# Retention with a snake feed-forward layer: one table for all steps, and the second projection of blocks 1 to 8 as seven products of quarters

## The chip, the cores and the metric

The kernel runs on 1 core of one Trainium2 chip. The metric is the device time of one execution in microseconds (us). Three runs of the kernel before took 311.48, 315.2 and 309.82 us, so the median is 311.48.

In this text TensorE (PE in the profile) does the matmuls, VectorE (DVE), ScalarE (ACT) and GpSimd (POOL) the rest, SyncE (SP) issues most transfers. PSUM is the memory that matmuls write, in eight banks of 128 partitions x 512 f32; SBUF is the working memory.

## The reference

The first part is causal retention per batch (8) and head (8) over 576 positions with 64 columns per head; the second a feed-forward layer over all 4608 rows.

```
scores = (q @ k.T) / sqrt(64)
rel = pos[:, None] - pos[None, :]
Dmat = where(rel >= 0, gamma[head] ** rel, 0)       # gamma = 1 - 2 ** (-5 - head)
x = ((scores * Dmat) @ v), heads side by side       # (4608, 512)
h = x @ w_in                                        # w_in (512, 2048)
s = sin(alpha * h)
g = h + s * s / (alpha + 1e-9)
out = g @ w_out                                     # w_out (2048, 512), out f32
```

## The kernel before

**Blocks.** The 4608 rows are nine blocks of 512. Blocks 0 to 7 are the first 512 positions of one batch each; block 8 gathers the last 64 positions of all eight batches (class `Ends`, L427).

**Retention of a block** (class `Attention`, L240). q, k and v come in two parts of 256 positions each (`load`, L109; 0.5 MB each, issued by SP; k and v of batches 5 to 7 in four DMAs a part). `cast` (L132) scales by powers of gamma and writes f16. q and k are turned, on TensorE with `turn`/`take` (L195, L208) in batches 0 and 1, by a transposing DMA (`crossed`, L187) in the others. A part has two chunks of 128 positions. `outer` (L269) makes each chunk's sum of k x v, `take_sum`, `evict` or `evict_bank` copy it out of PSUM, `more` (L320) and `to_state` (L315) carry the state from chunk to chunk. `scores` (L332), `masked` (L350), `values` (L362) and `add_states` (L395) make the rows of a part, `keep` (L413) copies them to the block's f16 tile `xT`. The matmuls here are 64x64 tiles that share the array. The two halves of `values` take turns at a PSUM bank; between them stands a marker instruction on another engine (`told`, L234).

**Feed-forward of a block.** Units are the 16 slices of 128 of the 2048 columns. `project` (L511) makes one unit of h: four matmuls, 512 columns each, into one bank. `sine` (L524) is ScalarE's activation from that bank, `square` (L532) runs on ScalarE, VectorE or POOL, `product` (L541) is VectorE's `g = ss * (1/alpha) + h`, reading the bank again, into the tile `gT` (f16, two buffers). So a bank of h is free only after `product`.

The second projection is `gemm2` (L557). Of its 16 row-and-quarter steps per block, four make one chunk of 128 output rows: 16 matmuls of 128x128 weights (a piece of `gT`) and 512 columns of `w_out`, accumulated in one bank. `finish` (L551) copies the chunk to SBUF and issues two stores.

```
def gemm2(n, u, tag, cols=slice(0, 512)):
    c, part = divmod(u, 4)
    ...
    for fk in range(4 * part, 4 * part + 4):
        matmul(
            ops[n, c, cols.start][:, cols], gT[n][:, fk, c * P : (c + 1) * P], w_out16[:, fk, cols],
            start=(fk == 0), stop=(fk == FC - 1), skip_group_check=True,
        )
```

The inner part of the loop from block 3 on (`todo` and `after` hold the retention steps and loads of each unit):

```
for u in range(16):
    project(n, u, next(h))
    sine(n, u)
    for f in todo.get(u, []):
        f()
    ...
    elif u % 4 == 3:
        gemm2(n - 1, u, "op")
        finish(n - 1, u // 4)
        square(n, u, A_)
        product(n, u)
    else:
        square(n, u, A_ if A and u in (ON_A if n < 4 else (4, 5, 8, 9, 10)) else V)
        product(n, u)
        gemm2(n - 1, u, "op")
```

**Order.** Every engine runs its instructions in the order in which the program issues them, and the order is written by hand (`with tc.manual_schedule()`, L619). Up to block 2 it is a straight list of calls; from block 3 on a loop over units (L1104 to L1191) runs `project(n, u)`, `sine`, `square`, `product` and one step of `gemm2(n - 1, u)`, with the next batch's retention and loads hung in at fixed units. After the loop the last block's second projection stands alone, its last chunk in two column pieces, copied by ScalarE and VectorE and stored through two queues. PSUM banks are named: `h0`, `h1`, `h2` for units, `op` for output chunks, `m0` and `m1` (two banks each) for retention and, early on, for units.

**Start.** The weights (4 MB each in f32) come through POOL's queue in four parts each (`load_w_in`, L89; `load_w_out`, L93) and are cast to f16 on the way. Before the first data is there, TensorE runs idle matmuls on zeros (`keep_busy`, L572).

Of the kernel before, what the change touches and what calls it, by code (L numbers as in the profile page):

```python
# [10 lines left out]
F32 = mybir.dt.float32  # L11
F16 = mybir.dt.float16
ADD = mybir.AluOpType.add
MULT = mybir.AluOpType.mult


@with_exitstack
def kernel(
# [10 lines left out]

# [9 lines left out]
    NBLK = NT // 512  # L44
    HALVED = 5
# [19 lines left out]
    work = ctx.enter_context(tc.tile_pool(name="w", bufs=1))  # L65
    psum = ctx.enter_context(tc.tile_pool(name="p", bufs=1, space=bass.MemoryType.PSUM))

    ident = const.tile([P, P], F16, tag="ident", bufs=1)
    mask = const.tile([P, 8 * 64], F16, tag="mask", bufs=1)
    cn = const.tile([P, 68], F32, tag="cn", bufs=1)  # L70
# [3 lines left out]
    eye = const.tile([16, 16], F32, tag="eye", bufs=1)  # L74
    alpha_r = const.tile([FC, P], F32, tag="alpha_r", bufs=1)
    alpha_t = const.tile([P, FC], F32, tag="alpha", bufs=1)
    inva = const.tile([P, FC], F32, tag="inva", bufs=1)
    w_in16 = const.tile([P, KT, FF], F16, tag="w_in16", bufs=1)
    w_out16 = const.tile([P, FC, 512], F16, tag="w_out16", bufs=1)
    sS = const.tile([P, B, 4, D], F16, tag="sS", bufs=1)  # L80
    xS = const.tile([P, KT, 512], F16, tag="xS", bufs=1)
# [4 lines left out]

    V, A_, G_ = nc.vector, nc.scalar, nc.gpsimd

    def load_w_in(g):  # L89
        cols = slice(g * 512, (g + 1) * 512)  # L90
        nc.gpsimd.dma_start(w_in16[:, :, cols], w_in_r[:, :, cols])

    def load_w_out(g):  # L93
        nc.gpsimd.dma_start(w_out16[:, 4 * g : 4 * g + 4, :], w_out_r[:, 4 * g : 4 * g + 4, :])
# [4 lines left out]
    def copy(eng, d_, s_):  # L99
        if eng is nc.scalar:  # L100
            eng.copy(d_, s_)  # L101
        else:
            eng.tensor_copy(d_, s_)  # L103

    raw = {}
    half = {}
    T = {}

    def load(b, nm, p):  # L109
        if p < 2 and b >= HALVED and nm != "q":  # L110
            t_ = work.tile([P, H, 2 * D], F32, tag="raw", bufs=6, name=nm + "32")
            for g in range(2):
                for r in range(2):
                    s0 = 256 * p + 128 * g + 64 * r
                    nc.sync.dma_start(  # L115
                        t_[halves(g), :, r * D : r * D + D], src[nm][b, :, s0 : s0 + 64, :].rearrange("h i d -> i h d")
                    )
        elif p < 2:
            t_ = work.tile([P, H, 2 * D], F32, tag="raw", bufs=6, name=nm + "32")
            nc.sync.dma_start(  # L120
                t_, src[nm][b, :, 256 * p : 256 * p + 256, :].rearrange("h (i r) d -> i h (r d)", r=2)
            )
        else:
            if b % 2 == 0:
                raw[b, nm, 2] = work.tile([P, H, D], F32, tag="raws", bufs=3, name=nm + "s32")
            t_ = raw[b - b % 2, nm, 2]
            nc.sync.dma_start(t_[halves(b % 2)], src[nm][b, :, 512:576, :].rearrange("h i d -> i h d"))
        raw[b, nm, p] = t_

    nbuf = {"k": 4, "q": 3, "v": 4}  # L130

    def cast(b, nm, p, eng, ys=(0, 1)):  # L132
        t_ = raw[b, nm, p]
        if (b, nm, p) not in half:
            if p < 2:
                d_ = work.tile([P, 16 * D], F16, tag=nm + "16", bufs=nbuf[nm], name=nm + "16")
                d_ = (
                    d_.rearrange("p (h r d) -> p h r d", r=2, d=D)
                    if nm == "v"
                    else d_.rearrange("p (a r t d) -> p a r t d", a=4, r=2, t=2)  # L140
                )
            elif nm == "v":
                d_ = work.tile([P, H, D], F16, tag="vs16", bufs=B // 2, name="vs16")
            else:
                d_ = work.tile([P, 4, 2, D], F16, tag="qks16", bufs=2, name=nm + "s16")
            half[b, nm, p] = d_
        dst = half[b, nm, p]
        if p == 2:
            if nm == "v":
                copy(eng, dst.rearrange("p h d -> p (h d)"), t_.rearrange("p h d -> p (h d)"))  # L150
            else:
                eng.tensor_tensor(  # L152
                    dst.rearrange("p a t d -> p t a d"),
                    t_.rearrange("p (t a) d -> p t a d", t=2),
                    fac_s[nm].rearrange("p (t a) -> p t a", t=2).unsqueeze(3).to_broadcast([P, 2, 4, D]),
                    MULT,
                )
        elif nm == "v":
            h0, h1 = 4 * ys[0], 4 * ys[-1] + 4
            copy(  # L160
                eng,
                dst[:, h0:h1].rearrange("p h r d -> p (h r d)"),
                t_[:, h0:h1].rearrange("p h x -> p (h x)"),
            )
        else:
            a0, a1 = 2 * ys[0], 2 * ys[-1] + 2
            n = 2 * (a1 - a0)
            eng.tensor_tensor(  # L168
# [44 lines left out]
    def quads(firsts, seconds):  # L213
        return [(f, s) for s in seconds for f in firsts]
# [1011 lines left out]
```

## Time and profile before

| | |
|---|---|
| span of the profiled execution | 309.4 us |
| runs | 309.82, 311.48, 315.2 us |
| TensorE busy | 296.4 us, 96% |
| VectorE, ScalarE, POOL busy | 207.4, 180.7, 138.4 us |
| first projection, first of block 1 | 25.4, 54.5 us |
| last matmul starts | 305.8 us |
| read from HBM | 36.74 MB |

The page gives the span from the first to the last instruction; the runs' times hold in addition what lies around it, at least 0.4 us here. A group line reads: line, engine, operation, output and inputs with shapes, count, then busy time and the mean duration in ns, then the engine's idle time before it with what ended it. A matmul's duration contains a tail that overlaps the next matmul; the distance from start to start is what it costs. A timeline line begins with start and length in us. A line of the stretches has the length, then busy us and instruction count of PE, weight load, DVE, ACT and POOL, then the granted clock, the share of the DMA engines and GB/s.

### The profile page before, as it was taken

To read this page: it belongs to the slowest core of one execution; us is meant where nothing else is said; L and a number is where in the kernel's file an instruction comes from. 1 tells how busy PE (TensorE), PEld (TensorE's weight loads), DVE (VectorE), ACT (ScalarE), POOL (GpSimd) and SP (SyncE) were. 2 spreads that over 40 slices of the span, in tenths; PEclk is the share of its full clock that TensorE was granted. 3 is DMA by queue.
4 is the path that set the end of the run, shared out by engine and by line. 5 is a ranking of instruction groups with operands and counts; after the bars stand their busy time and mean duration, and the time that the engine had idled before them with its cause. 6 is when DMAs were issued, how large, how long until landed. Compare 5 with 4: busy or idle time off the path is not lost.

```text
span 309.4 us, 7922 instructions
## 1 busy us (share of the span) xinstructions
PE 296.4 (96%) x3257; PEld 150.9 (49%) x3257; DVE 207.4 (67%) x298; ACT 180.7 (58%) x286; POOL 138.4 (45%) x154
## 2 busy tenths in 40 slices
PE   6669999999999999999999999999999999999995
PEld 4546555554544544454445444544454454444443
DVE  1596799989859888666866586576656746655600
ACT  1434983766544766675677567756774456555411
POOL 5690774589449587759149722990030000000000
PEclk9776999999999999999999999999999999999999
DMA  7999999699497788987788788885431111111132
GB/s 227 335 215 217 278 260 247 160 247 303 90 289 213 88 190 183 272 140 171 161 226 209 179 163 192 230 199 132 101 72 39 34 36 36 35 34 37 42 89 73
DMA packets 115540, 49.84 MB, mean 161 GB/s; under 512 B 69792, under 2 KB 111024, under 8 KB 115504
## 3 DMA queue, kind: packets, MB, share of 16 engines
q1 hardware_dynamic: 110912, 44.97, 60.0%
q0 software_dynamic: 4224, 4.19, 8.1%
q8 instruction: 25, 0.41, 0.6%
q10 hardware_dynamic: 368, 0.18, 0.3%
q14 instruction: 11, 0.09, 0.1%
HBM read 36.74 MB, written 9.44 MB: 149 GB/s over the span
## 4 chain that ended last, share of the span: by engine, by line
PE 84%; DMA 3%; POOL 3%; SPq 3%; DVE 2%; ACT 1%; issue 1%; DVEq 0%; ACTq 0%; POOLq 0%
PE ops L562 39%; PE hps L519 37%; DMA q<-in_q_dram 3%; PE o L384 3%; PE sc L342 2%; SPq L115 2%; POOL q L168 1%; PE kv L282 1%; DVE s L316 1%; DVE ret L354 1%; PE o L406 1%; SPq L120 1%; ACT s_t L527 1%; POOL k L168 1%; PE tr L201 0%
## 5 line engine op out<-in xcount | busy, mean ns | idle before, releaser
L562 PE MATMUL ops<-w_out,gT 128*128 128x512 f16 (+2 forms) x592 | 142.4, 374 | 0.3 <-ACT kvs L101 0.2
L543 DVE SCALAR_TENSOR_TENSOR gT<-ss_t,inva,hps 128x512 f16<-128x512 f16 x144 | 106.2, 745 | 53.1 <-ACT ss_t L536 46.1
L527 ACT ACTIVATE s_t<-hps,alpha_t 128x512 f16<-128x512 f32 x144 | 97.1, 686 | 71.3 <-PE hps L519 68.8
L519 PE MATMUL hps<-xT,w_in 128*128 128x512 f16 (+1 forms) x544 | 127.7, 370 | 0.0
L519 PEld LDWEIGHTS <-w_in 128*128 128x128 f16 x608 | 59.1, 99 | 64.5 <-issue 0.9
L562 PEld LDWEIGHTS <-gT 128*128 128x128 f16 x592 | 56.2, 98 | 64.3 <-issue 0.7
L538 DVE TENSOR_TENSOR ss_t<-s_t 128x512 f16<-128x512 f16 x72 | 42.2, 587 | 19.5 <-ACT s_t L527 18.8
L536 ACT ACTIVATE ss_t<-s_t 128x512 f16<-128x512 f16 x62 | 38.8, 631 | 0.9
L354 DVE TENSOR_TENSOR ret<-sc,mask 128x1024 f16<-128x1024 f32 (+1 forms) x32 | 35.1, 1118 | 1.9 <-PE sc L342 1.8
L168 POOL TENSOR_TENSOR k<-k,cn 128x1024 f16<-128x1024 f32 (+1 forms) x13 | 22.1, 1699 | 25.0 <-DMA k<-in_k_dram 20.7
L101 ACT COPY osb<-ops 128x512 f32<-128x512 f32 (+1 forms) x34 | 19.7, 582 | 22.0 <-PE ops L562 20.6
L168 POOL TENSOR_TENSOR q<-q,cn 128x1024 f16<-128x1024 f32 (+1 forms) x16 | 27.2, 1708 | 10.1 <-DMA q<-in_q_dram 10.0
L538 POOL TENSOR_TENSOR ss_t<-s_t 128x512 f16<-128x512 f16 x10 | 10.8, 1083 | 19.5 <-ACT s_t L527 10.7
L101 ACT CAST xT<-o 128x1024 f16<-128x1024 f32 (+1 forms) x14 | 13.2, 958 | 7.9 <-PE o L406 7.8
L324 POOL TENSOR_TENSOR kvs<-s,kvs 128x256 f32<-128x256 f32 x22 | 16.1, 730 | 3.1 <-ACT kvs L101 1.4
L103 POOL CAST v<-v 128x1024 f16<-128x1024 f32 (+1 forms) x10 | 12.2, 1234 | 9.5 <-DMA v<-in_v_dram 8.4
L519 PE MATMUL hps<-xS,w_in 128*128 128x512 f16 x64 | 16.4, 379 | 0.0
L323 POOL TENSOR_TENSOR s<-kvs,cn 128x256 f32<-128x256 f32 x22 | 14.3, 651 | 0.3
L152 POOL TENSOR_TENSOR ks<-ks,cn 128x512 f16<-128x512 f32 x4 | 4.2, 1041 | 22.0 <-PE o L384 22.0
L384 PE MATMUL o<-ret,v 64*64 64x128 f16 (+1 forms) x512 | 11.9, 226 | 1.3 <-DVE ret L354 0.7
L342 PE MATMUL sc<-qT,kT 64*64 64x128 f16 (+1 forms) x512 | 10.9, 221 | 1.9 <-DVE ret L354 1.9
L316 POOL TENSOR_TENSOR s<-kvs,cn 128x256 f16<-128x256 f32 x19 | 12.2, 646 | 1.1 <-ACT kvs L101 0.5
(59 smaller groups left out, 142.3 us busy)
## 6 DMA issues: line engine op xcount, KB each, us to landing
out_dram<-osb SPq DMA_DIRECT2D x70, 128.0 KB, 2.4
q<-in_q_dram SPq DMA_DIRECT2D x16, 512.0 KB, 6.2
k<-in_k_dram SPq DMA_DIRECT2D x10, 512.0 KB, 8.2
v<-in_v_dram SPq DMA_DIRECT2D x10, 512.0 KB, 6.2
k<-in_k_dram SPq DMA_DIRECT2D x24, 128.0 KB, 3.1
v<-in_v_dram SPq DMA_DIRECT2D x24, 128.0 KB, 3.2
w_in<-in_moe_w_in_dram POOLq DMA_DIRECT2D x4, 512.0 KB, 11.3
w_out<-in_moe_w_out_dram POOLq DMA_DIRECT2D x4, 512.0 KB, 9.8
```

The source lines that it names most:

```text
L101: eng.copy(d_, s_)
L168: eng.tensor_tensor(dst[:, a0:a1].rearrange("p a r t d -> p t (a r) d"), t_.rearrange("p (t a) x -> p t a x", t=2)[:, :, a0:a1].rearrange( ...
L324: nc.gpsimd.tensor_tensor(self.kvs[:, c], s32, self.kvs[:, c], ADD)
L342: matmul(sc[halves(g), t, c : c + n], kT[halves(t), 2 * a + r, halves(g)], qT[halves(t), 2 * a : 2 * a + 2, 64 * g + i0 : 64 * g + 64], st ...
L354: nc.vector.tensor_tensor(ret.rearrange("p t (z x) -> p (t z) x", z=2)[:, :, 0:n], sc.rearrange("p t (z x) -> p (t z) x", z=2)[:, :, 0:n], ...
L384: made.append(matmul(o[t][halves(e), c : c + 128].rearrange("p (r i) -> p r i", r=2)[:, :, i0:64], v16[halves(g), 4 * t + 2 * x + e, r, :] ...
L519: matmul(hps_of[n, fc][0][:, cols], w_in16[:, a, fc * P : (fc + 1) * P], xs[n][:, a, cols], start=(a == 0 and part != 1), stop=(a == KT - ...
L527: nc.scalar.activation(s_t, hps, mybir.ActivationFunctionType.Sin, bias=0.0, scale=alpha_t[:, fc : fc + 1],)
L536: nc.scalar.activation(ss_t, s_t, mybir.ActivationFunctionType.Square)
L538: eng.tensor_tensor(ss_t, s_t, s_t, MULT)
L543: nc.vector.scalar_tensor_tensor(gT[n][:, fc, :], ss_t, inva[:, fc : fc + 1], hps, MULT, ADD)
L562: matmul(ops[n, c, cols.start][:, cols], gT[n][:, fk, c * P : (c + 1) * P], w_out16[:, fk, cols], start=(fk == 0), stop=(fk == FC - 1), sk ...
```

## The change

**The table.** The calls, the loop and the tile pools are replaced by one text, `STEPS`, of 1542 steps in order. Each names an operation, its indices and, after a colon, its engine; `what=place` gives the new tile its PSUM bank or SBUF place by number, `<` adds a wait. So order, engines and places come from the table alone. PSUM is one tile of eight banks, SBUF four arrays of places (16 of 1024 f32, 28 of 1024 f16, 16 of 512 f16, two of `gT`).

```diff
+        for step in STEPS.replace("\n", ";").split(";"):
...
+            kind, *args = name.split(".")
+            args = [a if a in "qkv" else int(a) for a in args]
+            made = steps[kind](*args, *((E[eng],) if eng else ()))
+            done[name] = made
+            for w in words[1:]:
+                if w[0] == "<":
+                    order(made, done[w[1:]])
```

The steps keep the old operations under short names: LD load, CA cast, TU/TK turn and take, XP transposing DMA, OU/EV/TS sums and their evictions, MA/MB/ST states, SC/MK scores and mask, VA/RL/VB/SA values, marker, values, states, KP keep; PR project, SI sine, SQ square, PD product; KB idle matmuls; WI/WO weights; G2/FI/OS the old second projection, for block 0 only. All 144 projections are whole units of 512 columns; some of the first were two halves of 256 before. Squares are on ScalarE 108 times, POOL 19, VectorE 17 (62, 10, 72 before). The start of the table:

```
EY; MC; LD.0.q.0 raw.0.q.0=0; ZE; Z0; AR; LD.0.k.0 raw.0.k.0=1; KB.12.256.6; FS; CN; AT al=0; KB.15.256.6
LD.0.k.1 raw.0.k.1=2; AC:V; AI; CA.0.q.0.0:V q16.0.0=0; LD.0.q.1 raw.0.q.1=3; CA.0.q.0.1:V; TU.0.q.0.0 tr.0.q.0=0
...
LD.1.q.0 raw.1.q.0=7; WI.0; OU.0.0 kv.0.0.0=0 kv.0.0.1=2; KB.4.256.3; TS.0.1:A kvs.0=8; CA.0.q.1.1:V; TS.0.0:A
VA.0.0 o.0.0=6; KB.3.256.2; LD.1.v.0 raw.1.v.0=9; WI.1 <TS.0.0; RL.0.0:V; ST.0.0:V s16.0=10; TU.0.q.1.1; SA.0.0
```

**The seven products.** For blocks 1 to 8 the 512x2048 block of g and the 2048x512 `w_out` are cut into 2x2 quarters: 256 rows by 1024, and 1024 by 256 columns. With A of g and B of `w_out`, the output's quarters are made from seven products instead of eight:

```
S1 = A21 + A22   S2 = S1 - A11   S3 = A11 - A21   S4 = A12 - S2          (per block)
T1 = B12 - B11   T2 = B22 - T1   T3 = B22 - B12   T4 = B21 - T2, signs taken into the sums   (once)
P1 = A11 B11   P2 = A12 B21   P3 = S4 B22   P4 = A22 T4   P5 = S1 T1   P6 = S2 T2   P7 = S3 T3
```

The sums of g are `SM`, each in two halves of 128x1024 f16, eight instructions a block, on POOL (40 of 64) or VectorE (24). S1 and S4 overwrite A21 and A12. The sums of `w_out` are `TT`, eight instructions in all; T3 overwrites B12 after block 0 is done. A product is 16 matmuls of 128x128 weights and 256 columns in four groups of four (`PP`):

```diff
-    def gemm2(n, u, tag, cols=slice(0, 512)):
...
+    BANK_OF = {1: "X", 6: "X", 7: "X", 4: "X", 2: "Y", 5: "Z", 3: "Z"}
+
+    def PP(n, p, j):
+        ps = bank(f"{BANK_OF[p]}.{n}")
+        for u in (2 * j, 2 * j + 1):
...
+            for c in range(2):
+                i = matmul(
+                    ps[:, 256 * c : 256 * c + 256], left[:, 0, 128 * c : 128 * c + 128], right[:, 0, :],
+                    start=starts(f"{BANK_OF[p]}.{n}"), stop=True, skip_group_check=True,
+                )
+        return i
+
+    KEPT = {2: ("Y", "p2"), 6: ("X", "u2"), 7: ("X", "u3"), 4: ("X", "c21")}
+
+    def CP(n, p, eng):
+        b, t = KEPT[p]
+        return copy(eng, mid32(f"{t}.{n}"), bank(f"{b}.{n}"))
+
+    SUMS = {11: ("X", "p2"), 22: ("Z", "u3"), 12: ("Z", "u2")}
+
+    def AD(n, c):
+        b, t = SUMS[c]
+        return nc.vector.tensor_tensor(mid32(f"{t}.{n}"), bank(f"{b}.{n}"), mid32(f"{t}.{n}"), ADD)
```

Three banks of PSUM hold a block's products. X takes P1, then P6, P7 and P4 on top of it; `CP` copies Y and, after P6, P7 and P4, X to SBUF (27 of 32 on ScalarE). `AD` adds a bank to such a copy on VectorE: P1 + P2 for the first quarter of the output, Z after P5 for the fourth, Z after P3 on top for the second; the third quarter is the last copy of X. So before P6, P7 and P4 the bank X must have been read. `OQ` stores a quarter in two DMAs from SP, in runs of 256 columns (1 KB) where a chunk went in runs of 512. The table around block 1's sixth product (with units of block 2 and retention of batch 3 in between) and at its end:

```diff
+MK.3.0.1 ret.3.0.1=17; PP.1.1.3; SQ.2.3:A ss.2.3=10; MA.3.3:G s32.3.3=0; PR.2.5.2 hps.2.5=2; LD.4.q.1 raw.4.q.1=1
+SQ.2.4:A ss.2.4=11; ST.3.1:V; ST.3.2:G; LD.5.q.1 raw.5.q.1=7; AD.1.11; PR.2.6.2 hps.2.6=3; SI.2.5 s.2.5=7
+LD.5.k.0 raw.5.k.0=3; MB.3.3:G; PD.2.3; PP.1.6.2; SQ.2.5:A ss.2.5=13; CA.4.k.0.2:G k16.4.0=5; PD.2.4; PP.1.6.1
+SI.2.6 s.2.6=14; PP.1.6.3; PD.2.5; SQ.2.6:A ss.2.6=12; SC.3.1.0 sc.3.1.0=6; PR.2.7.2 hps.2.7=4; SI.2.10 s.2.10=4
+MK.3.1.0 ret.3.1.0=14; ST.3.3:G; XP.4.k.0 kT.4.0=22; SQ.2.10:A ss.2.10=0; PP.1.6.0; CA.4.q.0.2:G q16.4.0=27; PD.2.6
+PR.2.8.2 hps.2.8=0; CP.1.6:A u2.1=3; PD.2.10; SI.2.7 s.2.7=1; SC.3.1.1 sc.3.1.1=6; SI.2.8 s.2.8=3; PP.1.7.3
...
+PP.8.7.2; PP.8.7.3; PP.8.5.3; CP.8.7:A u3.8=9; PP.8.5.2; PP.8.4.1; AD.8.22; PP.8.4.3; PP.8.4.2; OQ.8.22.1; PP.8.4.0
+OQ.8.22.0; PP.8.3.2; CP.8.4:A c21.8=25; PP.8.3.1; OQ.8.21.0; PP.8.3.3; PP.8.3.0; OQ.8.21.1; AD.8.12; OQ.8.12.0
+OQ.8.12.1
```

1668 lines of the change are left out of this document (655 added, 1013 removed).

## Prediction

> **What bounds the kernel now.** I read the page's busy shares first, then the stretches, then the chain that ended last.
>
> ```profile
> span 309.4 us, 7922 instructions
> PE 296.4 (96%) x3257; PEld 150.9 (49%) x3257; DVE 207.4 (67%) x298; ACT 180.7 (58%) x286; POOL 138.4 (45%) x154
> ...
> 0.00:25.40 25.40, 16.74 (x328) 12.85 (x329) 14.83 (x17) 7.42 (x10) 17.51 (x29) 0.79 1.06 255
> 25.40:54.40 29.00, 28.66 (x363) 16.07 (x360) 24.35 (x45) 20.14 (x34) 15.60 (x17) 0.95 1.13 251
> 54.40:200.00 145.60, 145.25 (x1748) 71.82 (x1747) 109.09 (x147) 95.95 (x153) 94.29 (x95) 1.00 0.84 196
> 200.00:305.90 105.90, 105.70 (x826) 50.19 (x824) 58.80 (x91) 57.17 (x92) 10.97 (x15) 1.00 0.30 68
> ```
>
> After the stretch's length stand PE, weight load, DVE, ACT, POOL, the granted clock, the DMA share. From 25.4 us on TensorE has no idle time worth naming, and from 54.4 us on at the full clock; the other engines have a quarter or more to spare. So a column less in TensorE's stream is time won, as long as the others keep up. The first 25 us are different: the DMA share is at its ceiling and the clock is at 0.79.
>
> **The products.** What one matmul costs is its spacing, not its duration, which overlaps the next.
>
> ```profile
> 220.41 1.03 PE L519 MATMUL hps<-xT,w_in 128*128 128x512 f16 x4
> 221.27 1.03 PE L562 MATMUL ops<-w_out,gT 128*128 128x512 f16 x4
> ...
> L562 PE MATMUL ops<-w_out,gT 128*128 128x320 f16 x16 | 2.3, 300 | 0.0
> L562 PE MATMUL ops<-w_out,gT 128*128 128x192 f16 x16 | 1.5, 246 | 0.0
> L562 PEld LDWEIGHTS <-gT 128*128 128x128 f16 x592 | 56.2, 98 | 64.3 <-issue 0.7
> ```
>
> Four of 512 columns take 221.27 - 220.41 = 0.86 us: 0.216 each. Sixteen of 192 columns take 1.5 us with one tail of 0.246, so (1.5 - 0.25)/15 = 0.084; sixteen of 320, (2.3 - 0.30)/15 = 0.133. Halfway, 256 columns: 0.109, half of 0.216. Each has its own weight load, so a short matmul pays nothing extra. Blocks 1 to 8 hold 64 matmuls each, 512 x 0.216 = 110.6 us. The seven products of quarters are 16 matmuls of 256 columns each, 8 x 7 x 16 = 896, at 0.109: 97.7 us. **-12.9 us**; block 0 keeps the old form. At 0.108 it would be 13.8, at 0.112 10.2.
>
> **The start.**
>
> ```profile
> L91 POOL DMA_DIRECT2D w_in<-in_moe_w_in_dram x4: 746/803/932, 11.8 to 19.4; - x4
> DMA to landing us min/median/max: 8.2/11.3/12.1
> ...
> 25.44 3.27 PE hps L519 x12
> ...
> 54.54 4.39 PE hps L519 x28
> ...
> L562 PE MATMUL ops<-w_out,gT 128*128 128x512 f16 x36 | 8.6, 380 | 0.2 <-ACT kvs L101 0.2
> ```
>
> The first quarter of w_in lands at 11.8 + 8.2 = 20.0 us, the last at about 19.4 + 12.1 = 31.5, and the first projection starts at 25.4, at less than the full clock (12 matmuls, eight of them of 256 columns, in 3.27 us instead of 1.7). The table loads block 0's six parts first, issues the first w_in part behind three POOL casts (so it lands at about 20 again), and fills waits with 74 short idle matmuls that hold the clock. Projections can start at 20 to 21. Much of that is given back: the ninth unit needs the fourth w_in part, at 31. What remains is seen at the first projection of block 1, 54.5 us in the chain. Before it the old kernel has done 36 output matmuls (last row, 25.4 to 54.3 us), the new table 12 units of four, 48: 12 x 0.216 = 2.6 us more. In the new order that moment waits for block 1's last v part, behind 12 other parts of q, k and v (6.3 MB) and 8 MB of weights on a full DMA; I put it at 54, half a microsecond early. **-3 us**, with bounds 0 (v comes 3 us later, all given back) and -6 (25.4 - 20, all kept).
>
> **What is added on the other engines.**
>
> ```profile
> L543 DVE SCALAR_TENSOR_TENSOR gT<-ss_t,inva,hps 128x512 f16<-128x512 f16 x144 | 106.2, 745 | 53.1 <-ACT ss_t L536 46.1 <-POOL ss_t L538 3.9
> L354 DVE TENSOR_TENSOR ret<-sc,mask 128x1024 f16<-128x1024 f32 x20 | 23.7, 1218 | 1.9 <-PE sc L342 1.8
> L168 DVE TENSOR_TENSOR q<-q,cn 128x512 f16<-128x512 f32 x2 | 1.4, 690 | 5.7 <-DMA q<-in_q_dram 5.7
> L316 DVE TENSOR_TENSOR sS<-kvs,cn 128x256 f16<-128x256 f32 x1 | 0.4, 418 | 0.0
> L527 ACT ACTIVATE s_t<-hps,alpha_t 128x512 f16<-128x512 f32 x144 | 97.1, 686 | 71.3 <-PE hps L519 68.8 <-DVE ret L354 1.1 <-DVE gT L543 1.0
> L536 ACT ACTIVATE ss_t<-s_t 128x512 f16<-128x512 f16 x62 | 38.8, 631 | 0.9
> L101 ACT COPY osb<-ops 128x512 f32<-128x512 f32 x33 | 19.3, 587 | 20.4 <-PE ops L562 18.9 <-DMA k<-in_k_dram 0.2
> L168 POOL TENSOR_TENSOR q<-q,cn 128x1024 f16<-128x1024 f32 x12 | 22.9, 1916 | 10.1 <-DMA q<-in_q_dram 10.0
> ```
>
> Per block: eight half sums of 128x1024 f16 (64 in all, 40 on POOL, 24 on VectorE), three additions from PSUM (24, VectorE), and four evictions where four were. No row shows a 1024-wide f16 sum of two SBUF tiles. On POOL the 1024-wide f32 cast, 1.9, bounds it from above and half of that, by bytes, from below; I take 1.9, the row nearest in width and operands: 76 us more. On VectorE 512 f16 (0.42, next fence) and 256 f32 (0.418) cost the same, so time goes by bytes, and 1024 f16 costs what 512 f32 does, 0.69 (between 0.42 and 0.85). An addition of 512 from PSUM: 0.69 again. So VectorE gets 48 x 0.69 = 33 us, and gives away squares: 17 instead of 72. ScalarE takes 108 squares instead of 62: 46 x 0.631 = 29 us more. Counted over the whole table by such rows: VectorE 241 us, ScalarE 223, POOL 195, TensorE 279.
>
> Here lies the risk. In the stage from block 1's first projection to block 8's, the table gives TensorE 187 us (0.86 per unit, 0.436 per four short matmuls), VectorE 167, ScalarE 162, POOL 136. In this stage VectorE is no longer at 75% but at 89%, before any waiting, and its waiting is in the trace:
>
> ```profile
> 75.95 1.90 POOL L168 TENSOR_TENSOR q<-q,cn 128x1024 f16<-128x1024 f32 x1
> ...
> 76.72 1.42 DVE L538 TENSOR_TENSOR ss_t<-s_t 128x512 f16<-128x512 f16 x1 [0.18 <-ACT s_t L527]
> ...
> L538 DVE TENSOR_TENSOR ss_t<-s_t 128x512 f16<-128x512 f16 x34 | 24.0, 707 | 7.3 <-ACT s_t L527 6.8
> L538 DVE TENSOR_TENSOR ss_t<-s_t 128x512 f16<-128x512 f16 x28 | 12.5, 448 | 9.2 <-ACT s_t L527 9.0
> ```
>
> The square that starts at 76.72 is held until POOL's cast ends at 77.85 and is done 0.29 us later; its like take 0.42 with POOL quiet. The two groups are the same squares in 54 to 200 us, with POOL 65% busy, and in 215 to 300 us, with it nearly idle: 0.707 against 0.448, 0.26 us of waiting each. (The Trainium skill, "SBUF — State Buffer", section "Who interferes with whom", says that a VectorE instruction with two SBUF inputs and a GpSimd instruction that reads SBUF exclude each other for a whole instruction. The trace agrees, and the rule speaks against a change that adds 40 long POOL sums and 24 VectorE ones.) The stage holds 58 such VectorE instructions: 58 x 0.26 = 15, VectorE 182 of TensorE's 187. Full cover up to a mean wait of (187 - 167)/58 = 0.34 us.
>
> Where a stall comes first is bank X. Products 1, 6, 7 and 4 of a block accumulate in it in turn, and each eviction must be over before the next writes. Between them the table puts other matmuls, mostly two groups of four (0.87 us), in places 1.3 to 3.5. An eviction on ScalarE takes 0.59; behind one sine, 0.59 + 0.69 = 1.28. Ten of the 24 handovers have less than that: eight at 0.87, one at 0.44, one at 1.21: 8 x 0.41 + 0.84 + 0.07 = 4 us if a sine always stands ahead. **+4 us** for all stalls, bounds 0 and 16 (first rival). Waits added on queues: w_in's second part waits on POOL for block 0's first eviction, with two more w_in parts and a cast behind it; w_out's third and fourth wait for a state and a square; marks on ScalarE or VectorE wait for a group of value matmuls (0.2 to 0.4 us), with sines or products behind them. I cost them at nothing, for the loads queue on a full DMA anyway, and 16 marks at 0.4 each would be 6 us of two engines, within the bounds.
>
> **The end.**
>
> ```profile
> 305.87 0.36 DVE L103 COPY osb<-ops 128x192 f32<-128x192 f32 x1 [12.01 <-PE ops L562]
> ...
> L555 SPq DMA_DIRECT2D out_dram<-osb x72: 466/588/1954, 59.0 to 306.3; - x72
> ```
>
> The last eviction, 0.36 us, becomes an addition of 0.69, and its two stores both go through SP, the second 0.59 later, where two queues were used. The smaller stores (1 KB rows) run when the DMA share is 0.30. About +0.9, less what the old second queue cost: **+0.5 us**.
>
> **The sum**, against the span: 309.4 - 12.9 - 3 + 4 + 0.5 = 298.0. The runs shown are 309.82, 311.48 and 315.2: the median lies 2.1 over the span. Predicted: **300.1 us**.
>
> **The rivals.**
>
> *No change, ScalarE's order.* In 40 to 80 us of TensorE's work the table loads ScalarE with 41.7 us against 40.2. If at each of the 24 handovers an eviction stands behind one more activation than planned, 24 x 0.69 = 16.5 replaces the 4: 310.5, 312.6 as a median. For it: ScalarE is above TensorE for these 40 us. Against: it is at 81% afterwards, and most handovers have more cover than an eviction needs.
>
> *Slower, the shared access.* From block 1 on 69 two-SBUF instructions stand on VectorE with 197 us of its work, against 235 of TensorE. If each meets a POOL sum and waits half of it, 0.95, VectorE needs 197 + 66 = 262 and sets the end: +27.5, 321.5, as a median 323.6. It is slower than before from a mean wait of (235 + 15.4 - 197)/69 = 0.78. For it: POOL's instructions get longer. Against: 0.26 measured, and counting TensorE's time along the table, about a third of these instructions fall inside a POOL instruction, of VectorE's others 60%: the order seems to keep them apart.
>
> *More than predicted.* The start keeps its whole lead and nothing stalls: 309.4 - 12.9 - 6 + 0.5 = 291.0, median 293.1. Against it: the loads.
>
> That the products don't get shorter is hardly possible, by the spacings above.
>
> **Chances.** The forecast 0.70, with its own range 294 to 306; ScalarE's order 0.13; the shared access 0.09; more than predicted 0.08. The range 293 to 310 leaves out the slow rival, half of the fast one and some of the first. A measurement of this kernel tells about 2% from no change, 6.2 us: faster by more (below 305.3) 0.76, within 0.15, slower 0.09.
>
> **What would show it.** Right: short matmuls 0.109 apart; the first projection at 20 to 21 us; block 1's at about 54; PE gaps in the second stage 4 us together, ahead of writes to bank X and after an eviction; VectorE's SBUF sums above 0.69 only beside POOL. Wrong: a TensorE that idles for VectorE's gT products all along, sums on VectorE at 1.5 us or more, block 1's first projection after 57 us.

## The result and the profile after

The changed kernel took 326.85 us (median of four runs, 326.71 to 327.47), the kernel before 310.65 beside it on the same chip: a ratio of 1.059, 95% interval 1.053 to 1.066. The forecast was 300.1. The change made the kernel slower by 5 to 7%, where a gain of 3 to 4% had been forecast, and the one rival that forecast a slower kernel, the shared access, names another cause.

The page of the changed kernel, first its span and TensorE's line, then the stretches of the prediction (the last one is longer by the added time) and, behind the dots, two that are used with the experiments:

```profile
span 325.0 us, 8701 instructions
...
PE 295.7 (91%) x3599; PEld 185.9 (57%) x3599; DVE 255.2 (79%) x333; ACT 208.2 (64%) x335; POOL 215.7 (66%) x178
```

```profile
0.00:25.40 25.40, 20.27 (x332) 14.85 (x333) 17.08 (x25) 9.16 (x16) 14.26 (x29) 0.96 1.07 242
25.40:54.40 29.00, 27.34 (x293) 13.01 (x290) 28.57 (x40) 19.94 (x33) 19.78 (x18) 0.98 1.19 238
54.40:200.00 145.60, 130.62 (x1690) 78.30 (x1683) 120.28 (x145) 105.18 (x170) 119.42 (x92) 0.96 0.97 200
200.00:320.00 120.00, 117.22 (x1296) 79.75 (x1294) 88.61 (x125) 73.97 (x117) 62.23 (x42) 1.00 0.27 60
...
59.10:110.00 50.90, 41.33 (x492) 20.65 (x491) 38.16 (x45) 34.73 (x58) 41.05 (x36) 0.90 1.11 236
110.00:220.00 110.00, 102.11 (x1348) 66.42 (x1349) 92.72 (x117) 79.72 (x126) 85.58 (x61) 1.00 0.83 170
```

The third line is the one to compare. The kernel before had TensorE at 145.25 of 145.60 us there and the DMA share at 0.84; now TensorE stands for 15 us, the share is 0.97 and the clock 0.96. VectorE, ScalarE and POOL have idle time left, so none of them has become the bound.

**Did the products get shorter?** The timeline of TensorE in block 7's products, start and length in us:

```profile
276.40 1.04 PE L854 MATMUL banks<-w_out,g 128*128 128x256 f16 x8
277.27 0.60 PE L854 MATMUL banks<-r 128*128 128x256 f16 x4
277.71 0.60 PE L854 MATMUL banks<-r,g 128*128 128x256 f16 x4
278.19 1.02 PE L757 MATMUL banks<-r,w_in 128*128 128x512 f16 x4
```

Eight short matmuls take 277.27 - 276.40 = 0.87 us, 0.109 each, as forecast. Added up over the trace from start to start, where what clearly exceeds a matmul's usual spacing counts as a gap: the second projection fell from 124.4 to 111.8 us (-12.6; forecast -12.9). Idle matmuls on zeros grew from 4.5 to 8.6 (+4.1, all ahead of the first projection, in time that was gaps before), the rest is 0.6 less. Gaps grew from 24.6 to 48.2 us (+23.6), and from the last matmul's start to the end of the span it is 1.1 more. Sum: +15.6 = 325.0 - 309.4. Ahead of 60 us the gaps are 16.2 (17.7 before), behind it 32.0 (6.9 before). So the gain is there whole, and the loss is gaps, nearly all between 60 and 220 us.

**What TensorE waits for.** The timeline at the first big gap, TensorE's lines and then ScalarE's; in brackets the idle time ahead and what ended it:

```profile
68.68 2.11 PE L757 MATMUL banks<-r,w_in 128*128 128x512 f16 x9
70.72 0.42 PE L550 MATMUL banks<-h 64*64 64x128 f16 x16
73.77 2.88 PE L757 MATMUL banks<-r,w_in 128*128 128x512 f16 x8 [2.63 <-DVE g L776]
...
70.06 0.62 ACT L337 CAST h<-r 128x512 f16<-128x512 f32 x1 [3.53 <-DMA r<-in_v_dram]
70.58 1.84 ACT L764 ACTIVATE s<-banks,alpha 128x512 f16<-128x512 f32 x3
72.30 1.15 ACT L772 ACTIVATE s<-s 128x512 f16<-128x512 f16 x2
...
79.64 0.62 ACT L337 CAST h<-r 128x512 f16<-128x512 f32 x1 [2.90 <-DMA r<-in_v_dram]
```

TensorE's bracket names VectorE's gT product, as my "wrong" list had it. But a product needs its square and its sine, and these stand on ScalarE behind a cast of v, which waited 3.53 us for its data. At 79.64 the next cast waits again. The chain that ended last, from 59 to 110 us (first row: shares by line), with the queue that led to it:

```profile
by line: DMA r<-in_v_dram 28.5%; PE banks L757 10.9%; ACT s L772 10.8%; SPq L800 8.7%; ACT s L764 7.2%; issue 6.8%; PE banks L854 5.5%; ACT r L337 4.6%; SPq L432 4.6%; DVE h L537 3.9%; DVE h L563 2.4%; PE banks L550 1.9%; PE banks L506 1.3%
...
60.82 2.72 PE banks L757 x12
63.54 0.57 PE banks L550 x32
64.11 0.98 PE banks L757 x4
...
67.45 1.20 SPq L800
...
69.32 1.21 SPq L800
...
70.57 0.59 SPq L432
...
71.20 8.41 DMA r<-in_v_dram
...
92.33 6.14 DMA r<-in_v_dram
```

A load of batch 3's v is issued at 71.20 behind stores (L800) and other loads and lands 8.41 us later; batch 4's, issued at 92.33, takes 6.14. In the table the step that needs batch 3's k and v first (`OU.3.2`) stands behind 13 projections and 3 output steps from block 1's first projection on, 13.8 us of TensorE: 59.1 + 13.8 = 73, and the last v part landed at 79.6. The order asks for data that can't be there.

### The profile page after: what moved, and what is told of

Same layout as the page of the kernel before. It is cut to its first block, busy times and chain, and to the rows that moved or that the text cites. A ratio compares the mean times of both kernels' runs of the same rounds, so it can differ in the third digit from the quotient of the medians.

```text
span 325.0 us, 8701 instructions
## 1 busy us (share of the span) xinstructions
PE 295.7 (91%) x3599; PEld 185.9 (57%) x3599; DVE 255.2 (79%) x333; ACT 208.2 (64%) x335; POOL 215.7 (66%) x178
## 3 DMA queue, kind: packets, MB, share of 16 engines
HBM read 36.74 MB, written 9.44 MB: 142 GB/s over the span
## 4 chain that ended last, share of the span: by engine, by line
PE 50%; DVE 16%; DMA 10%; ACT 7%; SPq 6%; POOL 5%; issue 4%; ACTq 0%; DVEq 0%; POOLq 0%
PE banks L854 21%; PE banks L757 20%; DMA r<-in_v_dram 5%; DVE g L776 4%; ACT s L764 3%; DVE h L563 3%; ACT s L772 2%; PE banks L419 2%; DVE h L537 2%; DVE h L455 2%; PE banks L790 1%; POOL r L825 1%; PE banks L550 1%; DMA r<-in_q_dram 1%; DMA h<-in_v_dram 1%
## 5 line engine op out<-in xcount | busy, mean ns | idle before, releaser
L757 PE MATMUL banks<-r,w_in 128*128 128x512 f16 x576 | 142.3, 385 | 7.0 <-DVE g L776 7.0
L776 DVE SCALAR_TENSOR_TENSOR g<-s,inva,banks 128x512 f16<-128x512 f16 x144 | 103.3, 740 | 34.2 <-ACT s L772 25.8
L764 ACT ACTIVATE s<-banks,alpha 128x512 f16<-128x512 f32 x144 | 96.6, 684 | 41.5 <-PE banks L757 34.5
L854 PEld LDWEIGHTS <-g 128*128 128x128 f16 x640 | 61.5, 98 | 22.4 <-DVE g L776 2.2
L772 ACT ACTIVATE s<-s 128x512 f16<-128x512 f16 x108 | 66.6, 630 | 4.0 <-DMA s<-s 1.5
L854 PE MATMUL banks<-w_out,g 128*128 128x256 f16 x384 | 51.4, 273 | 1.9 <-DVE g L776 1.1
L837 POOL TENSOR_TENSOR r<-g 128x1024 f16<-128x1024 f16 x21 | 46.0, 2193 | 7.3 <-DVE g L837 4.5
L455 POOL TENSOR_TENSOR h<-r,cn 128x512 f16<-128x512 f32 (+1 forms) x28 | 42.6, 1526 | 12.3 <-DMA r<-in_q_dram 7.3
L337 ACT COPY h<-banks 128x512 f32<-128x512 f32 (+2 forms) x36 | 22.2, 619 | 32.3 <-PE banks L854 18.6
L563 DVE TENSOR_TENSOR h<-banks,mask 128x1024 f16<-128x1024 f32 (+1 forms) x32 | 35.1, 1115 | 2.5 <-PE banks L550 2.4
L837 POOL TENSOR_TENSOR g<-g,r 128x1024 f16<-128x1024 f16 x11 | 23.3, 2125 | 15.9 <-PE banks L854 14.5
L854 PE MATMUL banks<-r,g 128*128 128x256 f16 x256 | 33.1, 273 | 0.0
L773 POOL TENSOR_TENSOR s<-s 128x512 f16<-128x512 f16 x19 | 20.6, 1087 | 16.5 <-ACT s L764 15.6
L854 PEld LDWEIGHTS <-r 128*128 128x128 f16 x256 | 25.2, 100 | 10.4 <-issue 2.7
L870 DVE TENSOR_TENSOR h<-banks,h 128x512 f32<-128x512 f32 x24 | 16.3, 684 | 10.8 <-PE banks L854 10.4
L337 ACT CAST h<-r 128x512 f16<-128x512 f32 (+1 forms) x17 | 13.3, 792 | 17.7 <-DMA r<-in_v_dram 17.7
L837 POOL TENSOR_TENSOR g<-g 128x1024 f16<-128x1024 f16 x8 | 17.6, 2201 | 10.2 <-DVE g L776 10.1
L531 POOL TENSOR_TENSOR h<-r,cn 128x256 f32<-128x256 f32 x18 | 12.5, 694 | 8.3 <-DVE r L337 2.9
## 6 DMA issues: line engine op xcount, KB each, us to landing
w_in<-in_moe_w_in_dram POOLq DMA_DIRECT2D x4, 512.0 KB, 12.1
```

Source lines behind the costliest of these rows:

```text
L337: return eng.copy(d_, s_) if eng is nc.scalar else eng.tensor_copy(d_, s_)
L455: return eng.tensor_tensor(dst[:, a0:a1].rearrange("p a r t d -> p t (a r) d"), t_.rearrange("p (t a) x -> p t a x", t=2)[:, :, a0:a1].rea ...
L563: return nc.vector.tensor_tensor(ret(b, p, y).rearrange("p t (z x) -> p (t z) x", z=2)[:, :, 0:n], bank(f"sc.{b}.{p}.{y}", 2).rearrange("p ...
L757: i = matmul(ps[:, cols], w_in16[:, a, u * P : (u + 1) * P], x_of(n)[:, a, cols], start=starts(f"hps.{n}.{u}"), stop=(a == KT - 1), skip_g ...
L764: return nc.scalar.activation(small(f"s.{n}.{u}"), bank(f"hps.{n}.{u}"), mybir.ActivationFunctionType.Sin, bias=0.0, scale=alpha_t[:, u : ...
L772: return nc.scalar.activation(ss_t, s_t, mybir.ActivationFunctionType.Square)
```

## The experiments

Theory A: TensorE waits for the loads of later batches, which come late on a full DMA and a long queue and are asked for too early by the order. Theory B: the sums of quarters and the memory that VectorE and POOL share (my slow rival). Ratios are to the kernel before on the same chip; times of different chips differ by a per cent. All that isn't named is the changed kernel.

### Without the sums

```diff
     def SM(n, s, i, eng):
-        i *= 4
+        return None
...
-                6: lambda: (of_units(big16(f"S2.{n}"), u, 1), of_units(big16("T2"), u, 1)),
-                7: lambda: (of_units(big16(f"S3.{n}"), u, 1), quarter_b(0, 1, u, 1)),
+                6: lambda: (quarter_a(n, 1, 0, u, 1), of_units(big16("T2"), u, 1)),
+                7: lambda: (quarter_a(n, 0, 0, u, 1), quarter_b(0, 1, u, 1)),
```

> The 64 sums of g's quarters (8 per block) are left out; products 6 and 7 read quarters of g in their place, so TensorE has the same matmuls and the output is another. Theory A, late data (the table places casts of loaded parts before their loads can have come, with SP's queue and the DMA engines full, and each engine waits in order): little changes, 317 to 325 us as a median, because the loads stay where they are. Theory B, the shared access (the sums load VectorE and POOL, and each VectorE instruction with two SBUF inputs and each POOL instruction hold each other up): 40 sums of 2.2 us on POOL and 24 of about 1.1 on VectorE go, and the time falls to 305 or less.

322.7 us, ratio 1.046 (1.040 to 1.051). All 64 sums together, with every wait they cause, cost 4 us of the 16. Theory B falls as the main cause.

### Without the late loads

`held` is the set of places that have had a load before, so that something stands in them:

```diff
+            if kind == "LD" and int(args[0]) >= 3 and (True, place[f"raw.{name[3:]}"]) in held:
+                continue
+            if kind == "LE" and int(args[0]) >= 2 and (False, place[f"rs.{int(args[0]) // 2}.{args[1]}"]) in held:
+                continue
```

> The loads of q, k, v of batches 3 to 7 and most of those of the last 64 positions are left out; the casts read what the place held before, so these rows of the output are not the reference's. Every instruction of the compute engines stays. Theory A: with no data to wait for and SP's queue and the DMA engines relieved, the waits between 60 and 215 us go, some 15 to 25 us: 300 to 310. Theory B: nothing changes for VectorE and POOL: 320 to 327.

305.55 us, ratio 0.989 (0.985 to 0.993): 21 us less, all of the loss and more. Block 1's first projection hardly moves (58.6 for 59.1), block 3's comes at 109.8 instead of 124.2.

### Without the stores of blocks 0 to 7

```diff
+            if kind in ("OS", "OQ") and int(args[0]) < 8:
+                continue
```

> The 64 stores of the output of blocks 0 to 7 are left out (each 0.6 us of SP's queue and 128 KB), so those rows are not written. Theory A, with SP's queue as the place where the loads are late (stores that wait for their data stand ahead of loads): 40 us of SP's issue go before 215 us, and the time falls to 308 to 316. Theory A with the DMA engines alone as the place: 4 to 6 us at most, 320 to 323. Theory B: 325 to 327.

314.38 us, ratio 1.019 (1.011 to 1.028). Stores share SP's queue and the DMA with the loads; without them the loads come earlier (batch 3's last v part lands at 75.6 instead of 79.6) and 12.5 us come back.

### Casts of v on POOL

Thirteen steps as this one:

```diff
-CA.2.k.1.1:G; CA.2.v.0.0:A; VA.1.1 o.1.1=6; OS.0.0.0; G2.0.2.0; MA.1.3:V s32.1.3=11; RL.1.1:A; XP.2.k.0 kT.2.0=13
+CA.2.k.1.1:G; CA.2.v.0.0:G; VA.1.1 o.1.1=6; OS.0.0.0; G2.0.2.0; MA.1.3:V s32.1.3=11; RL.1.1:A; XP.2.k.0 kT.2.0=13
```

> The 13 casts of v of batches 2 to 7 that stand on ScalarE go to POOL at the same place in the order; the result stays the reference's. In the trace ScalarE waited 17.7 us for v to land with sines behind it. Theory A in the narrow form that this wait on ScalarE holds TensorE up: 315 to 321. Theory A in the wide form (TensorE needs the same data itself soon after, whatever engine casts it): 323 to 328. Theory B: POOL is loaded further, 327 to 335.

323.55 us, ratio 1.048 (1.043 to 1.053): 3 us. That the waiting cast blocks ScalarE's sines is true at 70 us, and yet a small part: taken off ScalarE, the wait reaches TensorE by another way, as the wide form of A has it. The timeline of this run, TensorE and POOL:

```profile
81.21 0.64 PE L506 MATMUL banks<-h 64*64 64x64 f16 x32 [3.93 <-POOL h L455]
...
78.98 1.17 POOL L337 CAST h<-r 128x512 f16<-128x512 f32 x2 [1.48 <-DMA r<-in_v_dram]
```

TensorE no longer stands for a product in 70 to 80 us; it stands 3.93 us in batch 3's `OU` itself, for a cast on POOL behind the cast of v, which waited for its data.

### Fewer issues, the same bytes

```diff
-HALVED = 5
+HALVED = 8
```

> The computation is whole. The keys and values of batches 5 to 7 are loaded as those of batches 0 to 4: one DMA for a part in place of four (12 parts, so 36 DMAs fewer on SP's queue, at 0.63 us each 22.7 us of SP's time between 93 and 184 us), with the same bytes; the score and value products of these batches get longer by what batches 0 to 4 pay (about 0.08 us a score step and 0.12 us a value step, some 2 us of TensorE in all, and 12 mask products by 0.26 us on VectorE). Theory A1 (data late because SP takes its issues one after the other): at least 6 us faster than the changed kernel, near 320 or below. Theory A2 (the table asks for the later batches' data before the transfers can bring it, and has TensorE stand for them, whatever SP's queue holds): within 3 us of the changed kernel, 324 to 330, with the longer products showing. Theory B (VectorE and POOL at the same memory): slower by 1 to 3 us.

321.12 us, ratio 1.041 (1.034 to 1.047), 5.7 us less by the ratios, just under the line I had drawn for A1. What the queue costs is seen on SP in the changed kernel, issue start and length:

```profile
118.79 0.62 SPq L874 DMA_DIRECT2D out_dram<-h  x1
119.46 2.67 SPq L428 DMA_DIRECT2D r<-in_v_dram  x4
122.17 0.64 SPq L642 DMA_DIRECT2D h<-in_v_dram  x1
122.86 1.80 SPq L874 DMA_DIRECT2D out_dram<-h  x2
124.70 2.68 SPq L428 DMA_DIRECT2D r<-in_k_dram  x4
```

From 115 to 211 us issue follows issue, the plain ones mostly at 0.60 to 0.67 us each. So the queue costs time of its own there, some 6 us.

### An eighth of the bytes, the same issues

`few` holds the names of the 48 loads of the run without them; the loads in four parts and those of the ends are cut in the same way:

```diff
+        m = 1 if f"LD.{b}.{nm}.{p}" in few else H
...
-            t_, src[nm][b, :, 256 * p : 256 * p + 256, :].rearrange("h (i r) d -> i h (r d)", r=2)
+            t_[:, :m], src[nm][b, :m, 256 * p : 256 * p + 256, :].rearrange("h (i r) d -> i h (r d)", r=2)
```

> Left out: seven of the eight heads in 48 loads (those of batches 3 to 7 and of the ends of batches 2 to 7), so the same DMAs are issued in the same order with an eighth of the bytes; everything else runs on what the places hold. Leaving these loads out as a whole gave 21.3 us; 36 issues fewer with the same bytes gave 5.7. If the bytes are what TensorE waits for, near the run without the loads: a ratio of 0.99 to 1.01 to the kernel before. If it is the issues on SP's queue, one after the other, a ratio of 1.04 to 1.06, as the changed kernel. Both in part: between, 1.01 to 1.04.

308.51 us, ratio 0.998 (0.994 to 1.002): some 19 of the 21 us. The stretches of this kernel that answer to the last two of the changed one:

```profile
59.10:110.00 50.90, 50.11 (x752) 29.24 (x751) 48.52 (x60) 45.49 (x75) 48.69 (x38) 1.00 0.58 112
110.00:220.00 110.00, 107.26 (x1335) 69.86 (x1334) 99.52 (x128) 82.59 (x131) 92.47 (x69) 1.00 0.48 93
```

From 59.1 to 110 us TensorE goes from 41.33 to 50.11 once the DMA share falls from 1.11 to 0.58. It is the bytes on a full DMA first and the issues second; the two runs overlap and don't add up.

### Neither late loads nor sums

The edits of the first two together.

> Left out: the 64 sums of quarters of blocks 1 to 8 (the sixth and seventh product read quarters of g in their place) and 48 loads, those of batches 3 to 7 and of the ends of batches 2 to 7; everything else runs on what the places hold. Alone, the sums gave 4.1 us and the loads 21.3. If the two are separate, 300 to 303 us. If the shared memory of VectorE and POOL is a second bound that the late loads hide (theory B behind A), 293 to 297: what my sum of the prediction had as 298 without a single sum. If the sums only mattered because late data had left no slack, 304 to 306.

303.9 us, ratio 0.985 (0.979 to 0.991), against 0.989 with the sums: with data in time they cost about 1 us. Even this kernel, with no sum and few loads, is not at the 300.1 that I gave the whole one: block 1's first projection is at 58.6 here too.

### The kernel before with small loads

The same cut in the kernel before, without the ends (30 loads), in two runs and a control. In the first its six tiles for loads are taken in strict turn, in the second the one that was read out first; the control is the second with whole loads.

```diff
+        m = 1 if b >= 3 and p < 2 else H
...
-            t_ = work.tile([P, H, 2 * D], F32, tag="raw", bufs=6, name=nm + "32")
+            t_ = wide.pop(0)
...
+            if read[b, nm, p] == 2:
+                wide.append(t_)
```

> This is the kernel before the change, with the loads of q, k and v of batches 3 to 7 (the 30 parts of 256 positions, not the ends) cut to one head of eight: the same DMAs, an eighth of the bytes; the tiles they go to are the same six in turn, declared one by one. Seven heads of these batches are left out so. In the new table an eighth of the bytes gave 6% back. If the late loads are a matter of the new order alone, the kernel before hides them and gains less than 1%: ratio 0.99 to 1.01. If the old kernel too waits for its loads, it gains as much as the new one, 3% or more, and the change would only have kept an old wait.

> The kernel before with the loads of the 30 parts of batches 3 to 7 cut to one head of eight (seven heads are left out), and with each load going to the tile that was read out first, of six. If the kernel before hides its loads, a ratio of 0.98 to 1.00 to the kernel before (the first 60 us, where the transfers are full with weights and batches 0 to 2, stay as they are). If it waits for them as the new table does, 0.97 or less.

> The kernel before, whole, only that the six tiles for loads are declared one by one and each load takes the one that was read out first. If the declaration changes nothing, a ratio of 0.99 to 1.01; if it brought the stall of the earlier run, 1.02 to 1.04.

The first missed: 317.24 us, ratio 1.028 (1.020 to 1.035), with one stall of 6.9 us at 79 us, where a cast of v waits for a load of k: in strict turn another load goes to its tile. It tells nothing of the bytes. The second: 308.91 us, ratio 1.000 (0.997 to 1.003), and the control 312.73, 1.010 (1.003 to 1.017). The stretch from 59.1 to 110 us, first of the kernel before, then of the second run:

```profile
59.10:110.00 50.90, 50.71 (x701) 25.39 (x699) 42.56 (x58) 29.90 (x48) 34.66 (x37) 1.00 0.87 208
59.10:110.00 50.90, 50.19 (x697) 25.14 (x696) 42.80 (x57) 29.77 (x48) 35.34 (x38) 1.00 0.55 117
```

So small loads give the kernel before nothing or, against the control, 1%: it hides its late loads. In the new table the cut gave 6%, and both kernels read the same 36.74 MB. It is what the table sets: the order, with the places and engines that go with it.

### Sorting the table anew

If the order is at fault, another order of the same 1542 steps must give the time back. First only SP's steps moved, then all:

> The computation is whole. Only the steps on SP's queue (loads, transposes, stores) have moved in the table, each to where the list has it earliest or latest without passing a step that shares its place; the other engines' order is that of the changed kernel. Theory A1 (the order of the queue alone is at fault, stores ahead of loads that are wanted sooner): 310 us or less. Theory A2 (the places come free and the data is asked for by the order of the other engines, so the queue has little room): 319 to 325.

> The computation is whole and every step of the table is there, the seven products and the sums among them; only the order of the steps, their places and for some the engine are others: sorted anew with the durations of the changed kernel's own trace, with 0.66 us for each issue on SP (1.36 for a transpose, 2.6 for a load in four parts), a load taken to land 3 to 5 us after its issue and later when others are ahead of it, and POOL's sums at 2.12 us. Theory A (late data is the cause, and it is the order's doing): under 305 us, with block 1's first projection near 55 us and the gaps of TensorE between 60 and 160 us gone. Theory B: what VectorE and POOL take from each other stays whatever the order, so above 315 us. If the seven products themselves cost more than they save, not below 310.

Both missed, on the slow side. Moving the queue alone: 331.92 us, ratio 1.075 (1.068 to 1.082). Loads of batch 3 that had moved ahead of batch 2's last v part held it up; it was issued at 56.91 instead of 51.11, landed 7.03 us later, and TensorE stood for 5.7 us at 59. All steps moved: 326.65 us, 1.059 (1.051 to 1.066). Here the sorting had put four loads of batches 3 and 4 among the first twelve in SP's queue and w_in's first part behind more casts on POOL (issued at 21.2 us instead of 13.1), and had not counted what that does to the start:

```profile
0.00:25.40 25.40, 18.53 (x282) 13.30 (x282) 12.01 (x20) 6.98 (x13) 15.23 (x27) 0.93 1.08 261
25.40:59.10 33.70, 27.34 (x265) 12.78 (x254) 24.93 (x31) 20.50 (x34) 22.15 (x26) 0.90 1.08 216
59.10:110.00 50.90, 48.87 (x691) 25.72 (x691) 45.56 (x63) 39.30 (x64) 25.54 (x28) 1.00 0.90 182
```

The third row, 48.87 for 41.33, is what A expects; the first two lose 12 us (block 1's first projection at 70.7). So the start was kept and the rest sorted again:

> The computation is whole, all steps of the table are there. The table up to block 1's first projection (its first 273 steps) is that of the changed kernel, word for word; behind it the order, the places and 164 engines are sorted anew, as in the first resorted table, which had lost its time in the start (block 1's first projection at 70.7 us, its weights issued later). Theory A (data late by the order of the table): block 1's first projection stays at 59, the gaps of TensorE between 60 and 220 us, 29.7 us in the changed kernel, fall to 5 to 12, and the time to 300 to 310 us. If the stalls come with the seven products whatever the order: 318 us or more, with the gaps where they were or elsewhere in the same sum.

313.16 us, ratio 1.013 (1.004 to 1.023). Block 1's first projection is at 58.9 and the gaps between 60 and 220 us fall from 29.7 to some 15. That is more than I gave it, and the trace shows a cost that I had not counted: 148 changes between matmuls of the whole array and the 64x64 ones of retention, two for each of the 74 stretches of retention (94 in the changed kernel, 62 in the kernel before). The rows at 60.82 in the chain of the changed kernel show it. Twelve matmuls of 512 columns take 2.72 us up to the start of the small ones, instead of 12 x 0.216 = 2.59; 32 small ones, 0.014 apart, take 0.57 instead of 0.45. Over the traces the change costs 0.09 us one way and 0.12 to 0.15 the other. (The Trainium skill, "TensorEngine Tiling (Array Packing)", section "Tiling Modes", says that changing the tiling mode drains TensorE; the trace agrees, with these times.) The last two tables were sorted with it:

> The computation is whole, all steps of the table are there. Kept as in the changed kernel are its first 170 steps, the loads of batches 0 to 2 and their order; behind them order, places and 191 engines are sorted anew, now also with what the trace shows for each change between the 128x128 matmuls and the 64x64 ones of retention on TensorE (0.093 us one way, 0.12 to 0.15 the other): 102 changes in place of 148 in the table sorted before (94 in the changed kernel). Theory A: block 1's first projection at 56 to 59, gaps of TensorE between 60 and 220 us below 10, and 298 to 307 us, a ratio of 0.96 to 0.99. If order can't do more than the last table did, 311 to 315.

> The computation is whole, all steps of the table are there. Kept are the first 110 steps and the loads of batches 0 to 2; the rest is sorted anew, with 92 changes between the 128x128 matmuls and the 64x64 ones (102 in the last table). If the order still holds time, block 1's first projection at 55 to 58 and 302 to 308 us, a ratio of 0.97 to 0.995. If what is left is the start (gaps of TensorE of 15 us and idle matmuls of 8.6 us in the first 60 us) and the changes, the same as the last one, 308 to 312.

309.56 us, ratio 1.004 (0.999 to 1.009), and 305.39 us, ratio **0.988 (0.984 to 0.992)**. The step `OU.3.2` stands in the changed kernel and in the last table in these rows:

```diff
-LD.4.v.0 raw.4.v.0=7; SI.1.12 s.1.12=8; VA.2.0 o.2.0=0; XP.3.k.1 kT.3.1=11; OU.3.2 kv.3.0=3 kv.3.1=5
+OU.3.2 kv.3.0=1 kv.3.1=3; SC.3.0.1 sc.3.0.1=6; EV.3.0:A kvs.3=9; OS.0.3.1; LD.4.v.1 raw.4.v.1=0; PP.1.5.2
```

ahead of the first are 13 projections of block 1 on, no product and 3 output steps of block 0 (13.8 us), ahead of the second 27, 19 and 1 (32.5 us). The stretches of the last table:

```profile
0.00:25.40 25.40, 20.04 (x332) 14.47 (x333) 16.48 (x25) 9.68 (x17) 13.94 (x28) 1.00 1.07 241
25.40:59.10 33.70, 31.54 (x361) 15.68 (x360) 30.93 (x45) 23.41 (x38) 12.70 (x16) 1.00 1.18 234
59.10:110.00 50.90, 50.70 (x780) 30.05 (x777) 47.28 (x64) 43.03 (x71) 38.87 (x39) 1.00 1.03 232
110.00:220.00 110.00, 108.15 (x1310) 70.12 (x1309) 100.21 (x142) 79.75 (x128) 63.82 (x57) 1.00 0.77 158
220.00:300.00 80.00, 77.25 (x824) 54.48 (x823) 64.58 (x93) 44.25 (x73) 31.19 (x21) 1.00 0.34 78
```

From 59.1 to 110 us the DMA moves 232 GB/s, as in the changed kernel (236), with the share still over 1, and TensorE works for 50.70 of 50.90 us: full transfers, hidden by the order. By the ratios this version is 1.2% under the kernel before (0.8 to 1.6%), a small gain, and 6.7% under the changed one. It isn't the order alone: the places are new and 191 steps have other engines, among them sums: VectorE does 47 of the 64 where it did 24. The sums in all cost the changed kernel 4 us; what the places add wasn't separated.

## Why the prediction was wrong

**What failed** is the term "+4 us for all stalls, bounds 0 and 16". I looked for stalls at bank X, between products and evictions. The gaps behind 60 us are 25.1 us above those of the kernel before (32.0 - 6.9). Of the loads the prediction said only that they "queue on a full DMA anyway", for marks and weights; it worked out block 1's last v part and no later one, and never set the time at which the table asks for batch 3 against the time at which its bytes can land, though the quoted DMA share of 1.13 up to 54 us was the sign. By removal, late loads are worth 21 us; the 4 us of gaps that are left are the size that I had given the term.

**Bank X** was named wrongly. Groups of TensorE by form; behind the bar busy us, mean ns, then idle us ahead by releaser:

```profile
L854 PE MATMUL banks<-w_out,g 128*128 128x256 f16 x384 | 51.4, 273 | 1.9 <-DVE g L776 1.1 <-DVE h L870 0.6
L854 PE MATMUL banks<-r,g 128*128 128x256 f16 x256 | 33.1, 273 | 0.0
L854 PE MATMUL banks<-r 128*128 128x256 f16 x128 | 17.2, 286 | 2.3 <-DVE h L870 1.9 <-POOL r L837 0.5
L854 PE MATMUL banks<-w_out,r 128*128 128x256 f16 x128 | 16.1, 273 | 0.2 <-ACT h L337 0.2
```

For the additions (L870) and copies (L337) that free a product's bank the products waited 0.6 + 1.9 + 0.2 = 2.7 us. The size of 4 would have held, had it been the only stall.

**The start**, -3, was wrong by about 5: block 1's first projection came at 59.1, not at 54, and the first projection of all at 25.2, not at 20 to 21. The view of w_in's four DMAs in the changed kernel, then pieces of its chain:

```profile
L402 POOL DMA_DIRECT2D w_in<-in_moe_w_in_dram x4: 746/775/942, 13.1 to 19.7; - x4
DMA to landing us min/median/max: 10.2/12.1/14.3
...
17.73 2.37 DVE h L537
21.16 1.22 DVE h L563
25.40 1.60 PE banks L757 x4
...
40.24 2.09 POOL r L825
45.44 2.58 POOL r L825
```

w_in's first part is issued at 13.1, not 11.8, and lands 10.2 us later, not 8.2: at 23.3. But the first projection doesn't wait for it. The chain to it runs through block 0's retention, a state (L537) and masks (L563) on VectorE, values, and the copy of the rows that the projection reads, done at 24.8. In the kernel before it was so too: w_in's first part landed at 20.0, and the projection came 5.4 us later. I took w_in for the release and left retention out. (A smaller slip: w_in's last part landed at 31.1 there, not 31.5; the 12.1 is another part's.) From the first projection to block 1's it took 33.9 us where it had been 29.0: 2.6 us for the 12 output matmuls more (counted rightly, 48 for 36) and 2.3 us more of gaps. The idle matmuls have no part in it (4 in this stretch, 0.4 us, as much as before). On the chain stand sums of `w_out` (L825), to which the prediction gave no price of their own; no run leaves them out, so what they cost isn't shown. Leaving out all late loads (58.6) doesn't change this moment.

**The products**, -12.9, were right: -12.6. **The end**, +0.5, was +1.1. The errors add up, with 25.1 of gaps where 4 stood: 0.3 + 5 + 21 + 0.6 = 27 = 325.0 - 298.0.

**The other engines.** VectorE's sums cost 0.69 us alone, as forecast, and up to 2.0 beside POOL; POOL's took 2.12, where I took 1.9 from a cast: 40 x 0.22 = 9 us more of POOL. Neither mattered much, since the sums in all cost 4 us.

**The rivals.** "No change, ScalarE's order" had the right engine to look at, but ScalarE stood for data and not for its load. "Shared access" forecast 323.6 and the kernel took 326.85; the nearness is chance, as the run without sums shows. No rival was built on late loads, and that is the second fault: the share and GB/s of every stretch were in the quoted rows.

**What stays open.** How the 21 us divide between bytes and issues can't be told exactly; one cut gives 19, the other 6, and they overlap. The last table stands 5.7 us of span above the 298.0 of the sum; its gaps (27.0 us in all) and idle matmuls (8.6) account for that, but whether they can be cut wasn't tried.

## What to carry to other kernels

When an order is made tighter, set each load's earliest landing (bytes ahead of it over the rate of the stretch, and issues ahead of it times the cost of one) against the time at which the new order asks for it, batch by batch, before costing anything on the engines. A DMA share near or above 1 that costs nothing now can be a wait that the order hides, and a new order can uncover it. A wait that the trace names on VectorE or ScalarE should be followed back through the queue of that engine until it ends at a transfer or at real work.

## What the runs showed of the hardware

A plain load or store took about 0.5 to 0.7 us of SP's queue each, 0.53 to 0.59 for 512 KB in the changed kernel and 0.44 to 0.58 for 64 KB in the run with an eighth of the bytes; a part in four DMAs of 128 KB took 2.67. A transposing DMA took about 1.3. While the DMA was full, single issues stretched to 7 us (from 19.5 to 41 us, beside the weights).

A change between whole-array and 64x64 matmuls cost 0.09 and 0.12 to 0.15 us, 0.2 us and more for each stretch of retention.

After a stall TensorE was slow for a while: the stretch from 59.1 to 110 us has a granted clock of 0.90. In the timeline above, the eight matmuls from 73.77 to 76.44 take 2.67 us instead of 8 x 0.216 = 1.73, since from 74.7 on they are 0.43 apart, up to 78.0. (The Trainium skill, "TensorE: Matmul & The Clock Gate", section "What's actually happening", puts the window after which an idle array falls to half its clock at about 3.4 us; here 2.63 us without a matmul, behind a short stretch of small ones, were enough.) Behind 50 us this adds some 3 us in the changed kernel and nothing in the last table, where the granted clock is 1.00 in all five stretches.
